# One load per tile over all partitions, the scores in two PSUM tiles, the last table products behind the first expert's products

## The chip, the cores and the metric

The kernel runs on one core of a Trainium2 chip. The metric is the time of one execution on the device in microseconds (us); the median of the runs counts. TensorE is PE in the profile, VectorE DVE, ScalarE ACT, GpSimd POOL; SyncE (SP) issues most transfers here.

## The reference

A causal linear attention with a decay per channel, then a mixture of experts with one expert per row and a skip gate. Cut to what matters:

```python
x = attention(q, k, v, alpha)      # B, H, S, D = 4, 8, 768, 48; x is 3072 x 384
for t in range(S):
    state = alpha[:, :, t, :, None] * state + np.einsum('bhd,bhe->bhde', k[:, :, t], v[:, :, t])
    y[:, :, t] = np.einsum('bhd,bhde->bhe', q[:, :, t], state)
...
do_compute = x @ w_skip > 0        # D, E, F = 384, 8, 1024
logits = x[do_compute] @ w_gate
e_idx = np.argmax(logits, axis=1)  # gate_w: the softmax value of that expert
...
for e in range(E):
    h = np.maximum(xc[e_idx == e] @ w1[e], 0.0)
    y[e_idx == e] = gate_w * (h @ w2[e])
out[do_compute] = xc + y           # all other rows: out = x
```

## The kernel before

**Tiles.** Attention is cut into 24 tiles (NT) of 128 tokens: tile i is chunk i // 4 of batch i % 4, with all eight heads. A tile lies in one of six buffers (`qkv0` to `qkv5`, NQ = 6) of 1932 floats per partition (TW): 524 of decays with guards (`alpha`, AW), 512 of k, 512 of q and 384 of v. For alpha, k and q two heads stand on partitions 0 to 47 and 64 to 111 (PD = 112 in all), four pairs of heads beside each other; v has its 128 tokens on the partitions.

**Loads.** `load` brings the first six tiles' alpha, k and q from `first` over 112 partitions, later ones from `tiles` in two transfers over 48 partitions each, and v in a transfer of its own. All are issued by SP in the order of the code, each waiting there until its part of the buffer is free, and so are the stores of x, the weight pieces (`raw`) and the copies of zeros.

**A tile's steps.** DVE scans the decays backward (`suffix`, `sfx`) and forward (`prefix`, `pfx`); POOL scales k and q by them (`scale_k`, `scale_q`). PE forms the scores (`scores`, 16 products into `ps_s`), half of which ACT copies out (`take_scores`) and POOL masks (`mask_left`), while DVE masks the other half as it copies it (`mask_right`). PE transposes k (`turn_k`, `ps_k`, copied by ACT to `kt`), and adds up y from the old state (`inter`), and from the scores and v (`intra`) in `ps_y`; `outer` and `carry` bring the state on (`ps_v`, then DVE). ACT copies y out as `xt` (`take_y`). One turn later PE multiplies xt by `xw` (`rows`), which gives x as rows and the nine logits (expert gates and skip) in `ps_g`; DVE reduces the logits (`take_logits`) and ACT copies x (`take_x`), which SP stores.

**Order.** Each engine runs its instructions in the order of the code; there is no planner. The loop of `attention` runs the stages of several tiles in one turn i: load i+5, store i-2, scores i+1, prefix and scale_q i+2, inter i, mask_right, turn_k and mask_left i+1, suffix i+3, rows, take_logits and take_x of i-1, scale_k i+3, outer, intra, carry and take_y i. Between them stand jobs that are dealt out in pieces: `route_group` (the routing of tiles 0 to 7, 8 to 14 and 15 to 19; its `one_hot` runs on ACT as two steps, `far` and `hot`, and its `marks` are products on PE that add each row's number and gate to the table `tab`), `weight_pieces` (SP loads w1 and w2 in pieces) and `split_pieces` (ACT rounds a piece to `w1h` or `w2h`, POOL subtracts it to get the rest, `w1l` or `w2l`).

**Tail.** Tiles 20 to 23 are routed one by one (`route_one`). The first expert's rows are gathered by products with one-hots (`late_rows`, `early_turn`) and copied to `xx` (`first_turn`). After that the last two tiles' one-hots, marks and table additions follow, then `indices` (row numbers for the gathers), the gates and the gathers (POOL, `xr`) for experts 1 and 0.

**Experts.** For each of eight experts `up` multiplies (72 products of `ps_h` in four groups), `turn` transposes the next expert's gathered rows (`ps_x`), and `down` multiplies back (48 products of `ps_o`), adds the gated result to x and scatters the rows. `must_redo` forms a flag from the decays that tells whether tiles must be computed again another way.

## Time and profile before

| | us |
|---|---|
| median of 3 runs | 315.44 (314.89 to 315.59) |
| the profiled execution | 314.29 |
| its span | 312.6 |
| PE, DVE, POOL, ACT busy | 284.1, 205.9, 151.3, 141.8 |

The span runs from the first to the last instruction of the profiled execution; 1.7 us lie around it. Its mean granted TensorE clock was 0.919 of full speed. Tile i's start can be read by the start of its scores on PE (line 254): tile 2 at 18.45 us, tile 12 at 67.62, tile 23 at 139.37; the experts begin at 163.76. Busy shares of the whole span are means over these stages and are to be read stage by stage.

### The profile page before, as it was taken

What the parts mean: (1) busy time and instruction counts of PE and PEld (TensorE: products, weight loads), DVE (VectorE), ACT (ScalarE), POOL (GpSimd) and SP (SyncE); (2) the same over time, 40 slices, a digit from 0 to 9 for tenths busy, and PEclk for the clock granted to TensorE, in tenths of its full rate; (3) what the DMA queues carried; (4) which work ended last, traced back from release to release, by engine and by line L of the source; (5) the groups of instructions that cost most, each with busy time, mean ns of one, the idle gap of its engine ahead of it and who ended that gap; (6) DMA issues with size and microseconds to landing.
All of it is one profiled execution on the core that took longest, in us unless ns stands there. A gap on an engine that the chain in (4) does not pass through costs nothing.

```text
span 312.6 us, 7251 instructions
## 1 busy us (share of the span) xinstructions
PE 284.1 (91%) x2831; PEld 265.9 (85%) x2831; DVE 205.9 (66%) x398; ACT 141.8 (45%) x290; POOL 151.3 (48%) x176
## 2 busy tenths in 40 slices
PE   8768999979889979978949999999999999999991
PEld 8557888868778768866939999999999999999991
DVE  5579878896554975884554667675867679575510
ACT  4222555554873567333313827264563817264200
POOL 6287888978676776655127160331414050301111
PEclk9857999995987997996778999999999999999998
DMA  7899999999998892534203355576664756660000
GB/s 203 219 249 199 261 242 282 214 206 229 259 257 228 187 230 86 173 126 113 99 26 97 123 178 206 219 262 226 226 227 130 235 189 209 226 226 25 11 26 21
DMA packets 22793, 55.88 MB, mean 179 GB/s; under 512 B 3896, under 2 KB 10621, under 8 KB 22752
## 3 DMA queue, kind: packets, MB, share of 16 engines
q1 hardware_dynamic: 20576, 50.27, 58.2%
q0 software_dynamic: 2176, 5.08, 4.8%
q8 instruction: 24, 0.39, 0.6%
q14 instruction: 17, 0.14, 0.2%
HBM read 48.30 MB, written 8.65 MB: 182 GB/s over the span
## 4 chain that ended last, share of the span: by engine, by line
PE 61%; DMA 18%; DVE 10%; ACT 4%; POOL 3%; issue 2%; SPq 1%; POOLq 0%; DVEq 0%; ACTq 0%
PE ps_h L633 23%; PE ps_o L648 21%; DMA qkv<-in_tiles_dram 9%; DVE sfx L214 4%; DMA qkv<-in_v_dram 3%; DMA out_dram<-x 3%; DMA qkv<-in_first_dram 3%; PE ps_s L254 3%; PE ps_y L311 2%; PE ps_g L338 2%; PE ps_y L291 2%; PE ps_x L613 1%; PE ps_v L466 1%; DVE pfx L224 1%; PE ps_k L275 1%
## 5 line engine op out<-in xcount | busy, mean ns | idle before, releaser
L653 POOL DMA_INDIRECT out_dram<-o,idx x16 | 22.8, 1424 | 97.6 <-DVE o L651 97.6
L633 PE MATMUL ps_h<-xx,w1h 128*128 128x256 f32 x384 | 59.7, 286 | 0.4 <-DVE tab L471 0.4
L633 PEld LDWEIGHTS ps_h<-xx,w1h 128*128 128x128 f32 x384 | 52.9, 194 | 0.5 <-issue 0.5
L637 ACT ACTIVATE hh<-ps_h 128x512 fp32r<-128x512 f32 x32 | 19.1, 597 | 71.0 <-PE ps_h L633 65.5
L648 PE MATMUL ps_o<-w2h,hh 128*128 128x384 f32 x128 | 43.4, 339 | 0.0
L648 PE MATMUL ps_o<-w2h,hl 128*128 128x384 f32 x128 | 42.9, 335 | 0.0
L648 PE MATMUL ps_o<-w2l,hh 128*128 128x384 f32 x128 | 42.8, 334 | 0.0
L230 POOL TENSOR_TENSOR qkv<-qkv,sfx 112x512 f32<-112x512 f32 x24 | 28.4, 1182 | 23.8 <-DVE sfx L214 21.7
L254 PE MATMUL ps_s<-qkv 48*128 48x128 f32 x384 | 31.3, 308 | 5.2 <-POOL qkv L234 2.8
L638 DVE SCALAR_TENSOR_TENSOR hl<-ps_h,hh 128x512 fp32r<-128x512 f32 x32 | 22.1, 691 | 20.1 <-ACT hh L637 19.1
L254 PEld LDWEIGHTS ps_s<-qkv 48*128 48x128 f32 x384 | 26.5, 210 | 10.2 <-issue 4.1
L633 PE MATMUL ps_h<-xx,w1l 128*128 128x256 f32 x192 | 34.9, 287 | 0.0
L214 DVE TENSOR_TENSOR_SCAN sfx<-qkv,ps_d 112x524 f32<-112x524 f32 x24 | 29.7, 1236 | 7.5 <-DMA qkv<-in_first_dram 6.1
L311 PE MATMUL ps_y<-st,qkv 128*48 128x128 f32 x384 | 33.0, 314 | 0.0
L268 DVE COPY_PREDICATED st<-mask,ps_s 128x512 f32<-128x512 uint8 x24 | 17.6, 734 | 22.3 <-ACT st L260 22.2
L651 DVE SCALAR_TENSOR_TENSOR o<-ps_o,gates,xr 128x384 f32<-128x384 f32 x16 | 9.9, 618 | 30.2 <-PE ps_o L648 30.2
L224 DVE TENSOR_TENSOR_SCAN pfx<-qkv,ps_d 112x524 f32<-112x524 f32 x24 | 29.6, 1234 | 0.1
L633 PEld LDWEIGHTS ps_h<-xx,w1l 128*128 128x128 f32 x192 | 28.7, 196 | 0.0
L349 ACT COPY x<-ps_g 128x384 f32<-128x384 f32 x22 | 10.5, 477 | 38.9 <-DVE ps_d L343 38.9
L338 PE MATMUL ps_g<-xw,xt 112*128 112x105 f32 x176 | 27.3, 305 | 0.8 <-ACT xt L318 0.8
L234 POOL TENSOR_TENSOR qkv<-qkv,pfx 112x512 f32<-112x512 f32 x22 | 26.1, 1186 | 2.6 <-DVE pfx L224 2.4
L586 DVE TENSOR_TENSOR w1l<-raw,w1h 128x768 fp32r<-128x768 f32 x28 | 26.8, 957 | 0.8
(162 smaller groups left out, 552.1 us busy)
## 6 DMA issues: line engine op xcount, KB each, us to landing
raw<-in_w_dram SPq DMA_DIRECT2D x64, 384.0 KB, 4.9
qkv<-in_tiles_dram SPq DMA_DIRECT2D x36, 290.2 KB, 8.9
qkv<-in_v_dram SPq DMA_DIRECT2D x24, 192.0 KB, 8.3
...
```

Of the source, the lines that this page charges most:

```text
L214: nc.vector.tensor_tensor_scan(sfx[:PD][:, ::-1], w["alpha"][:PD][:, ::-1], self.c_r[:PD].to_broadcast([PD, AW]), LOW, ALU.mult, ALU.max)
L224: nc.vector.tensor_tensor_scan(pfx[:PD], w["alpha"][:PD], self.c_f[:PD].to_broadcast([PD, AW]), 0.0, ALU.mult, ALU.max)
L230: (eng or self.nc.gpsimd).tensor_tensor(w["kh"][:PD], w["kh"][:PD], w["sfx"][:PD, :, 3:SEG], ALU.mult)
L234: (eng or nc.gpsimd).tensor_tensor(w["qh"][:PD], w["qh"][:PD], w["pfx"][:PD, :, 2:2 + P], ALU.mult)
L254: nc.tensor.matmul(self.ps_s[:, h, p * P:(p + 1) * P], lhsT=kh[r, p, :], rhs=qh[r, p, :], start=True, stop=True)
L311: nc.tensor.matmul(self.y_out(i, p, h), lhsT=w["v"][:, o:o + D], rhs=w["st"][:, h, p * P:(p + 1) * P], start=(i < B and p < 2), stop=(p >= 2))
L338: nc.tensor.matmul(pg[:, p, :], lhsT=w["xt"][:PD, p, :], rhs=self.xw[:PD, p, :], start=True, stop=True)
L586: (nc.gpsimd if early else nc.vector).tensor_tensor(lo[:, s], raw[:, s], hi[:, s].bitcast(F32), ALU.subtract)
L633: nc.tensor.matmul(ps[:, u, :], lhsT=a[:, k, f * P:(f + 1) * P], rhs=xx[:, k, b, :], start=(n == 0), stop=(n == len(order) - 1))
L638: nc.vector.scalar_tensor_tensor(out=hl, in0=ps, scalar=0.0, in1=hh.bitcast(F32), op0=ALU.max, op1=ALU.subtract)
L648: nc.tensor.matmul(ps, lhsT=a[:, f, js], rhs=b[:, f, :], start=(n == 0), stop=(n == 3 * FT - 1))
L653: ins = nc.gpsimd.indirect_dma_start(out=self.out[:, :], out_offset=bass.IndirectOffsetOnAxis(ap=self.idx[:, e, j:j + 1], axis=0), in_=o, ...
```

## The change

- **Loads.** One input `tiles` of 24 x 128 x 1932 floats, zero where no head lies. A tile is one transfer over 128 partitions, instead of three. At the start tile 0 comes in four pieces, tile 1 in three and tile 2 in two, tile 2's alpha ahead of tile 0's v.
- **Scores.** `ps_s` becomes two tiles of PSUM, one for each half of the scores.
- **Order in the loop.** `take_x` stands ahead of `take_logits`. `route_constants` moves from turn 1 to 3, and its DVE part, on PSUM instead of SBUF, to turn 5. The weight pieces of expert 0 are issued in even turns from 4 on instead of every turn from 3 on, its splits run from turn 9 instead of 6.
- **Tail.** The marks of the last two tiles, their addition to the table, the indices, the gates and the gathers stand in `finish_table`, behind the first quarter of the first expert's products, with `all0` and `all1` as the one-hots.
- **Small.** `must_redo` takes one set of operations over 112 partitions instead of two; the sum of a group's counts lies in PSUM; `hot` has five buffers instead of six.

```diff
@@ -99,7 +99,7 @@
         bank = st.enter_context(tc.tile_pool(name="bank", bufs=1, space=PSUM))
-        self.ps_s = bank.tile([P, 2, NP * P], F32, name="ps_s")
+        self.ps_s = [bank.tile([P, NP * P], F32, name=f"ps_s{h}") for h in range(2)]
         self.ps_y = bank.tile([P, 2, 4 * P], F32, name="ps_y")
@@ -165,11 +165,6 @@
         nc.gpsimd.tensor_copy(self.slots, num)
-        nc.vector.tensor_copy(self.iota, self.slots)
-        self.rank = const.tile([P, E], F32, name="rank")
-        for t in (self.rank, self.rev):
-            nc.vector.tensor_scalar(out=t, in0=self.slots[:, 0:E], scalar1=-1.0, scalar2=float(E + 1),
-                                    op0=ALU.mult, op1=ALU.add)
         self.m = const.tile([P, NT, E], BF16, name="m")
@@ -182,6 +177,15 @@
+    def route_constants_2(self):
+        nc = self.nc
+        nc.vector.tensor_copy(self.iota, self.slots)
+        self.rank = self.const.tile([P, E], F32, name="rank")
+        for t in (self.rev, self.rank):
+            nc.vector.tensor_scalar(out=t, in0=self.iota[:, 0:E], scalar1=-1.0, scalar2=float(E + 1),
+                                    op0=ALU.mult, op1=ALU.add)
     def warm_up(self, n):
@@ -198,14 +202,8 @@
                                 qh=cut(QO, NP * P).rearrange("p (a t) -> p a t", t=P), v=cut(VO, DM))
-        for a, b in cuts or ((0, VO), (VO, TW)):
-            if a == VO:
-                nc.sync.dma_start(out=t[:, VO:], in_=self.v[i])
-            elif i < NQ:
-                nc.sync.dma_start(out=t[:PD, a:b], in_=self.first[i, :, a:b])
-            else:
-                for h in range(2):
-                    nc.sync.dma_start(out=t[64 * h:64 * h + D, a:b], in_=self.tiles[i - NQ, h, :, a:b])
+        for a, b in cuts or ((0, TW),):
+            nc.sync.dma_start(out=t[:, a:b], in_=self.tiles[i, :, a:b])
@@ -251,13 +249,13 @@
                 r = slice(64 * h, 64 * h + D)
-                nc.tensor.matmul(self.ps_s[:, h, p * P:(p + 1) * P], lhsT=kh[r, p, :], rhs=qh[r, p, :],
+                nc.tensor.matmul(self.ps_s[h][:, p * P:(p + 1) * P], lhsT=kh[r, p, :], rhs=qh[r, p, :],
                                  start=True, stop=True)
...
         w = self.work[i]
-        self.nc.scalar.copy(out=w["st"][:, 0, :], in_=self.ps_s[:, 0, :])
+        self.nc.scalar.copy(out=w["st"][:, 0, :], in_=self.ps_s[0])
@@ -413,16 +411,16 @@
         yield nc.vector.tensor_reduce(out=r1, in_=eq, op=ALU.add, axis=AX.X)
-        add = self.sm.tile([P, E], F32, name="add")
+        add = self.ps_d[:, 224:224 + E]
         yield nc.vector.tensor_reduce(out=add, in_=m.rearrange("p n e -> p e n"), op=ALU.add, axis=AX.X)
-        yield nc.vector.tensor_tensor(self.cnt, self.cnt, add, ALU.add)
+        yield nc.vector.tensor_tensor(self.cnt, add, self.cnt, ALU.add)
         w = n if g1 == LATE else 4
...
                 yield
-            ps, Vq = self.ps_v[:, 192:192 + 2 * 3 * E], V[:, q:min(q + w, n), :]
+            ps, Vq = self.ps_v[:, 192:192 + 2 * 3 * E], [V[:, k, :] for k in range(q, min(q + w, n))]
             yield from self.defer(lambda: self.marks(ps, hots, Vq))
@@ -439,16 +437,22 @@
         n = g1 - g0
-        V = self.sm.tile([P, 8, 3 * E], F32R, name="V")[:, :n, :]
+        if g0 >= LATE:
+            V = self.x0.tile([P, 1, 3 * E], F32R, name=f"V{g0}")
+        else:
+            V = self.sm.tile([P, 8, 3 * E], F32R, name="V")[:, :n, :]
         self.nc.gpsimd.tensor_tensor(V.rearrange("p n (e c) -> p n e c", c=3),
...
-    def one_hot(self, r1, eng=None):
-        nc = self.nc
-        hot = self.sm.tile([P, CAP], F32R, name="hot", bufs=6)
+    def one_hot(self, r1, eng=None, late=None):
+        nc = self.nc
+        if late is None:
+            hot = self.sm.tile([P, CAP], F32R, name="hot", bufs=5)
+        else:
+            hot = self.x0.tile([P, CAP], F32R, name=f"all{late % 2}")
         if eng is not None:
@@ -515,10 +519,10 @@
         yield
-        hot = self.one_hot(r1, nc.vector)
+        w["mark"] = [self.one_hot(r1, nc.vector, i)], [V[:, 0, :]]
         yield
         ps = w["pg"][:, 436:436 + 2 * 3 * E]
-        yield from self.defer(lambda: self.marks(ps, [hot], V))
+        yield from self.defer(lambda: self.marks(ps, *w["mark"]))
         yield self.add_marks(ps)
@@ -601,6 +605,17 @@
         self.ew.setdefault(e, {}).update(xr=xr)
+    def finish_table(self):
+        ps = self.ps_f.tile([P, 2 * 3 * E], F32, name="ps_f")
+        self.marks(ps, *self.last_marks)
+        self.add_marks(ps)
+        self.idx = self.indices(0, E, "idx")
+        for n in (1, 0):
+            self.gather(n)
+        self.gate = self.const.tile([P, NB, E], F32, name="gates")
+        self.nc.vector.tensor_tensor(self.gate, self.tab[:, :, :, 1], self.tab[:, :, :, 2], ALU.add)
@@ -864,9 +877,9 @@
         self.load(0, (0, AW), (KO, QO), (QO, VO))
-        self.load(1, (0, AW))
+        self.load(1, (0, AW), (KO, VO))
+        self.load(2, (0, AW))
         self.load(0, (VO, TW))
-        self.load(1, (KO, VO))
         self.constants()
@@ -877,7 +890,8 @@
         self.load(1, (VO, TW))
-        for i in range(2, NQ - 1):
+        self.load(2, (KO, TW))
+        for i in range(3, NQ - 1):
             self.load(i)
@@ -898,14 +912,14 @@
                 self.store(i - 2)
-            if i == 3:
+            if i == 4:
                 fetch = self.weight_pieces(0)
...
                 fetch = self.weight_pieces(1)
-            advance(fetch, 1 if i < 19 else 2)
+            advance(fetch, 2 if i >= 19 else 1 if i % 2 == 0 else 0)
             if LATE <= i + 5 < NT:
                 self.clear(i + 5)
-            if i == 6:
+            if i == 9:
                 split = self.split_pieces(0, early=True)
@@ -922,14 +936,16 @@
             self.tick(2)
-            if i == 1:
+            if i == 3:
                 self.route_constants()
+            if i == 5:
+                self.route_constants_2()
             if i + 3 < NT:
...
                 self.rows(i - 1)
+                self.take_x(i - 1)
                 self.take_logits(i - 1)
-                self.take_x(i - 1)
             if i + 3 < NT:
@@ -956,7 +972,7 @@
         a, b = NT - 2, NT - 1
-        self.x0t = [self.ps_s[:, 0, :CAP], self.ps_s[:, 1, :CAP], self.ps_v[:, 256:256 + CAP]]
+        self.x0t = [self.ps_s[0][:, :CAP], self.ps_s[1][:, :CAP], self.ps_v[:, 256:256 + CAP]]
         for i in range(LATE, a):
@@ -980,22 +996,15 @@
         advance(solo[a - 1], 2)
-        advance(solo[a], 6)
-        advance(solo[b], 7)
-        self.flush()
-        advance(solo[a], 2)
-        advance(solo[b], 2)
-        self.idx = self.indices(0, E, "idx")
-        self.gate = self.const.tile([P, NB, E], F32, name="gates")
-        nc.vector.tensor_tensor(self.gate, self.tab[:, :, :, 1], self.tab[:, :, :, 2], ALU.add)
+        advance(solo[a], 5)
+        advance(solo[b], 6)
+        self.last_marks = [self.work[a]["mark"][n] + self.work[b]["mark"][n] for n in range(2)]
         advance(fetch, 8)
...
         self.ew[0] = dict(xx=self.xx0)
-        for n in (1, 0):
-            self.gather(n)
         for e in range(E):
@@ -1003,6 +1012,8 @@
                 self.up(e, g)
+                if (e, g) == (0, 0):
+                    self.finish_table()
                 advance(split)
@@ -1037,16 +1048,15 @@
     tiles[:, :, :D, QO:VO] = heads(q).reshape(NT, 2, D, NP * P)
-    first = tiles[:NQ].reshape(NQ, P, VO)[:, :PD]
-    tiles = tiles[NQ:, :, :D]
-    vt = v.reshape(B, H, C, P, D).transpose(2, 0, 3, 1, 4).reshape(NT, P, DM)
+    tiles = tiles.reshape(NT, P, TW)
+    tiles[:, :, VO:] = v.reshape(B, H, C, P, D).transpose(2, 0, 3, 1, 4).reshape(NT, P, DM)
     w9 = np.concatenate([moe_w_gate, moe_w_skip[:, None]], axis=1).reshape(NP, 2, D, E + 1).transpose(1, 2, 0, 3)
...
     w2 = moe_w2.reshape(E, FT, P, DM).transpose(0, 2, 1, 3).reshape(E, P, FT * DM)
-    return [np.ascontiguousarray(a) for a in (first, tiles, vt, w9, w1, w2, nat, w9n)]
+    return [np.ascontiguousarray(a) for a in (tiles, w9, w1, w2, nat, w9n)]
```

ACT around one tile's turn in the middle of the loop, before; a name behind "waits" is the engine or the transfer queue that the row waits for.

```order
L260 COPY st_103<-ps_s 128x512 [waits PE_49,Pool_49]
L238 COPY ends<-pfx 112x4 [waits DVE_49]
L277 COPY kt<-ps_k 128x448 [waits PE_49,Activation_49]
L349 COPY x<-ps_g 128x384 [waits DMAHW7_49,DVE_49]
L436 CAST idg<-gate 128x8
L585 CAST w1h<-raw 128x512 [waits DMAHW3_49]
L318 COPY xt_108<-ps_y 112x2x2x128 [waits PE_49,Activation_49]
```

After, on the same engine in the same place:

```order
L258 COPY st_104<-ps_s_90 128x512 [waits PE_49,Pool_49]
L236 COPY ends<-pfx 112x4 [waits DVE_49]
L275 COPY kt<-ps_k 128x448 [waits PE_49,Activation_49]
L347 COPY x<-ps_g 128x384 [waits DMAHW4_49,PE_49]
L434 CAST idg<-gate 128x8 [waits DVE_49]
L589 CAST w1h<-raw 128x512 [waits DMAHW2_49]
L316 COPY xt_109<-ps_y 112x2x2x128 [waits PE_49,Activation_49]
```

The copy of x (now line 347) waits for PE where it waited for DVE. DVE in the same place, before:

```order
L268 COPY_PREDICATED st_103<-mask,ps_s 128x512 [waits Activation_49]
L214 SCALAR_TENSOR_TENSOR sfx<-qkv_101,ps_d 112x524 [waits DMAHW7_49,DMAHW0_49,Pool_49]
L218 RECIPROCAL qkv_101<-sfx 112x4 [waits DVE_49]
L343 TENSOR_REDUCE ps_d<-ps_g 128x9 [waits PE_49]
L388 TENSOR_REDUCE mx<-ps_d 128x8 [waits DVE_49]
```

After, on the same engine in the same place:

```order
L266 COPY_PREDICATED st_104<-mask,ps_s_91 128x512 [waits PE_49]
L212 SCALAR_TENSOR_TENSOR sfx<-qkv_102,ps_d 112x524 [waits DMAHW0_49,Pool_49]
L216 RECIPROCAL qkv_102<-sfx 112x4 [waits DVE_49]
L341 TENSOR_REDUCE ps_d<-ps_g 128x9 [waits Activation_49]
L386 TENSOR_REDUCE mx<-ps_d 128x8 [waits DVE_49]
```

The logits' reduction (line 341) waits for ACT instead of PE, the mask (line 266) for PE instead of ACT, and the suffix scan for one transfer instead of two. PE at the end of the tail, before (`ps_g` and `ps_k` are the table products of the last two tiles, `ps_h` the first expert's):

```order
L466 MATMUL ps_g<-V,hot 128x24 [waits DVE_49,Pool_49]
L466 MATMUL ps_g<-V,hot 128x24
L466 MATMUL ps_k<-V,hot 128x24 [waits DVE_49,Pool_49]
L466 MATMUL ps_k<-V,hot 128x24
L633 MATMUL ps_h<-xx_2041,w1h 128x256 [waits DVE_49,Activation_49]
```

After, on the same engine in the same place:

```order
L533 MATMUL ps_v<-hot_1992,latel_1959 128x256
L648 MATMUL ps_h<-xx_2000,w1h 128x256 [waits DVE_49,Activation_49]
L648 MATMUL ps_h<-xx_2000,w1l 128x256
...
L648 MATMUL ps_h<-xx_2000,w1l 128x256
L648 MATMUL ps_h<-xx_2000,w1h 128x256 x6
L470 MATMUL ps_f<-V_2015,all_2017 128x24 [waits Pool_49]
L470 MATMUL ps_f<-V_2026,all_2028 128x24 [waits Pool_49]
L470 MATMUL ps_f<-V_2015,all_2017 128x24
```

The table products, four in `ps_f`, stand behind 18 of the first expert's products instead of ahead of them.

## Rows read from the trace of the kernel before

**Rows 1.** Windows: length; busy PE, PEld, DVE, ACT, POOL; clock; DMA share; GB/s.

```profile
7.30:35.30 28.00, 22.05 (x254) 19.26 (x254) 21.83 (x33) 8.31 (x21) 17.77 (x25) 0.76 0.98 223
35.30:62.70 27.40, 27.40 (x459) 23.82 (x458) 22.28 (x43) 15.07 (x35) 24.29 (x28) 1.00 1.04 250
62.70:139.40 76.70, 67.43 (x934) 58.55 (x933) 54.00 (x115) 43.38 (x104) 54.67 (x64) 0.89 0.80 202
...
163.80:306.00 142.20, 142.15 (x1004) 141.63 (x1004) 90.83 (x133) 65.14 (x102) 40.38 (x31) 0.99 0.49 167
```

**Rows 2.** Chain of waits at the start: start, duration, what.

```profile
8.67 5.71 DMA qkv<-in_first_dram
14.40 1.26 DVE sfx L214
...
18.45 2.08 PE ps_s L254 x16
```

**Rows 3.** Timeline, DVE and PE at 23 to 32 us: start, duration, engine, line.

```profile
23.83 2.20 DVE L171 TENSOR_SCALAR rank<-slots 128x8 f32<-128x8 f32 x1
...
25.81 1.58 PE L254 MATMUL ps_s<-qkv 48*128 48x128 f32 x16
...
31.27 1.16 PE L254 MATMUL ps_s<-qkv 48*128 48x128 f32 x16
```

**Rows 4.** Waits, 62.7 to 139.4: who for whom: total us, times, longest.

```profile
ACT x L349 <- DVE ps_d L343: 21.6, 12, 2.8
DVE st L268 <- ACT st L260: 15.4, 9, 3.1
...
PE ps_y L291 <- ACT xt L318: 7.5, 7, 1.7
```

**Rows 5.** Timeline, 68 to 117 us; in brackets idle before, and its releaser.

```profile
68.78 0.48 ACT L349 COPY x<-ps_g 128x384 f32<-128x384 f32 x1 [2.82 <-DVE ps_d L343]
...
70.41 0.66 PE L291 MATMUL ps_y<-qkv,old 48*48 48x128 f32 x16 [1.63 <-ACT xt L318]
...
91.09 0.69 PE L291 MATMUL ps_y<-qkv,old 48*48 48x128 f32 x16 [1.43 <-ACT xt L318]
...
116.60 0.66 PE L291 MATMUL ps_y<-qkv,old 48*48 48x128 f32 x16 [1.68 <-ACT xt L318]
```

**Rows 6.** Windows at the half clock between 62.7 and 139.4 us.

```profile
71.10:77.90 6.80, 6.80 (x63) 6.22 (x65) 4.86 (x10) 2.45 (x5) 5.38 (x7) 0.50 1.04 224
91.60:98.40 6.80, 6.80 (x64) 6.14 (x58) 3.73 (x6) 2.98 (x7) 6.32 (x8) 0.50 0.84 218
118.90:122.30 3.40, 3.40 (x33) 3.21 (x34) 2.53 (x7) 2.27 (x6) 2.19 (x4) 0.50 0.00 0
```

**Rows 7.** Windows by transfers: stores and v, then 48-partition loads alone.

```profile
99.00:100.00 1.00, 1.00 (x23) 0.81 (x15) 0.43 (x1) 0.64 (x2) 0.39 (x1) 1.00 0.88 320
101.00:103.00 2.00, 2.00 (x39) 1.87 (x38) 1.90 (x7) 0.48 (x1) 0.73 (x1) 1.00 1.08 223
```

**Rows 8.** Groups by line, ACT, 62.7 to 139.4: busy us, mean ns, idle before.

```profile
L585 ACT CAST w2h<-raw 128x512 fp32r<-128x512 f32 x6 | 3.6, 608 | 0.0
```

**Rows 9.** Timeline of the tail, 159 to 165 us.

```profile
159.10 0.42 DVE L550 CAST xx<-ps_s 128x256 fp32r<-128x256 f32 x1 [1.30 <-ACT xx L550]
...
161.83 0.47 DVE L453 TENSOR_SCALAR hot<-ps_d,r 128x256 fp32r<-128x256 f32 x1
...
162.76 0.60 PE L466 MATMUL ps_k<-V,hot 128*128 128x24 f32 x2 [0.25 <-DVE tab L471]
...
164.31 1.04 POOL L556 DMA_INDIRECT xr<-out_dram,idx  x1 [1.60 <-DVE gates L990]
```

**Rows 10.** Chain of waits at the first expert.

```profile
163.76 10.14 PE ps_h L633 x72
...
173.90 0.66 PE ps_x L613 x6
```

**Rows 11.** Gathers of xr between 163 and 172 us, from issue to landing.

```profile
DMA to landing us min/median/max: 3.7/3.7/3.7
```

28 lines of the change are left out of this document (13 added, 15 removed).

## Prediction

> **What bounds the kernel now.** I read the windows by stage first, because the share of busy time over the whole span (PE 91%) mixes stages with different limits. [rows 1] shows four stretches. In the first, 7.30 to 35.30, PE works 22.05 of 28.00 us and the DMA share is 0.98: the pipeline fills and is fed by transfers. From 35.30 to 62.70 PE works all 27.40 us (six tiles, 4.57 us each): nothing but PE counts there. From 62.70 to 139.40 it works 67.43 of 76.70, at a mean granted clock of 0.89. From 163.80 on, the experts, it works 142.15 of 142.20. So only the first and third stretch, and the short tail ahead of 163.8, can give time back by better feeding.
>
> Then the chain of waits for the first stretch [rows 2]: the load of tile 2 is issued at 8.67 and takes 5.71 us; tile 2's suffix scan starts as it lands (14.40), and scan, scaling and scores follow, so that PE's scores of tile 2 start at 18.45. Then the timeline there [rows 3]: two operations of 8 columns keep DVE 2.20 us from 23.83, ahead of tile 4's suffix scan, and the scores of tiles 3 and 4 start 31.27 - 25.81 = 5.46 us apart.
>
> Then the waits of the third stretch [rows 4]: ACT idles 21.6 us ahead of its copy of x for DVE's logits, DVE 15.4 us ahead of its mask for ACT's copy of the scores; they wait for each other although neither needs the other's result. PE's own large wait is that for xt, ACT's last copy of a tile: 7.5 us in seven times. [rows 5] shows the link: at 68.78 ACT starts x after 2.82 us idle, and 1.6 us later PE starts `inter` after waiting 1.63 us for xt. The last two rows there are two more of the seven. [rows 6] shows what follows: three stretches at 0.50 of the full clock (1.2 instead of 2.4 GHz), beginning 0.7, 0.5 and 2.3 us after those three waits ended, PE busy throughout. 17.0 us at half speed hold 8.5 us of work, so they cost 3.4 + 3.4 + 1.7 = 8.5 us.
>
> **The change part by part.**
> *The loads.* A tile was 2 x 297 KB over 48 partitions and 197 KB over 128; it is 989 KB over 128 partitions, 198 KB more, 24 x 198 KB = 4.75 MB in all, with one issue instead of three. Rates: while loads over 48 partitions ran alone, 223 GB/s at a share of 1.08; with the share at 0.88 in a microsecond of transfers over 128 partitions, 320 [rows 7]. In the PE-bound stretch the new need is 989 KB, a store and on average one weight piece of 197 KB each, 1,383 KB per 4.57 us = 303 GB/s. The new loads resemble the second row, so 320 to 360 are there and I charge nothing; with the first row's rate it is the first rival.
> The Trainium skill ("SBUF — State Buffer", section "Door 1: The DMA port swizzle (why `[64,N]` ≈ `[32,N]`)") says that a transfer's rate goes by how many of 16 ports its partitions reach, and 48 partitions of one half reach eight. An estimate from that page would be 594/218 + 197/435 = 3.2 us per tile before and 989/435 = 2.3 after; the 223 GB/s row agrees with its first half, no row here shows the second for a whole load.
> A load now also waits for v's reader, `intra` of the tile before, one loop turn ahead; the five spare buffers cover that: nothing, and 5.71 us once if not.
> *The start.* The decays of tile 2 are now loaded ahead of the first v. Their scan no longer starts at 14.40 but when DVE is done with tiles 0 and 1, at about 11.2; 14.40 to 18.45 is 4.05 us of scan, scalings and scan, which gives scores at 15.2, or 16.8 if k and q, in the second transfer, come last. Gain 1.7 to 3.2, I take 2.8. The constants move out: tile 4's scan loses up to 2.2 us of delay; the interval falls from 5.46 toward the steady 4.57, and a little below it if tile 3 comes later than that scan allowed before: 0 to 2.2, I take 1.5. Start **4.3 (1.7 to 5.4)**. The constants' DVE part goes to loop turn 5, where DVE works 22.28 of 27.40 us and PE has a full queue [rows 1]: nothing; without that cover 2.2.
> *x ahead of the logits.* ACT's copy of x waits for PE instead of DVE; DVE's reduction waits for ACT instead of PE. Queued behind ACT's copy are routing one-hots, the weight splits (0.608 us) [rows 8] and xt, so xt comes earlier by as much as ACT was kept idle just before. Of PE's 7.5 us the five waits with such idle time ahead can go by 0.3, 1.5, 0.75, 0.3 and 0.9, about 3.7; the other two, one of them behind one-hots, stay. Range 2 to 6. Queued behind DVE's new wait are the state update, the next prefix scan and the next mask, for which `inter` and the scores wait; ACT stood ready for that copy in 12 cases, 21.6 us in all [rows 4], so nothing, at worst one x copy of 0.48 us [rows 5] in each of 12 tiles: 6.
> *Scores in two tiles of PSUM.* Removes DVE's 15.4 us of waiting; DVE is not what PE waits for there and has 22.7 us to spare, so nothing by itself: the work it hides behind is PE's.
> *The clock.* With the waits at 70.41, 91.09 and 116.60 shortened to some 0.1, 0.7 and 0.8 us, the first half-clock stretch has lost the wait that stood ahead of it, the others half of theirs. Between 0 and 8.5 I count one: 3.4.
> *Weights later.* Splits run in turns 9 to 20 instead of 6 to 17: three more fall where the one-hots of the second and third group crowd ACT, 0.6 us of ACT each [rows 8], and some of POOL. 0 to 3.2 lost; I take 1.2.
> Middle: 3.7 + 3.4 - 1.2 = **5.9 (0 to 12)**.
> *Late and tail.* For the last tiles the logits now come one x copy later, 0.48 [rows 5]: -0.4. The last one-hot starts at 161.83 and ends at 162.30, the table products take 0.60 a pair [rows 9] and the first expert's products start at 163.76 [rows 10]. These no longer stand behind the table, which saves 1.46; DVE's copy for them at 159.10 waited 1.30 for ACT's, of which 0.42 go. But the two pairs now run inside the PE-bound stage: 1.9 - 1.2 = 0.7. The gathers were issued from 164.31, 0.55 after the products' start. Now 18 of 72 products come first (2.5 us by 10.14/4, twice that at the half clock, I take 3.8), 1.2 of table products and the 0.95 from their end to the issue: 5.9 after. The second, 1.04 on, lands 3.7 later [rows 11], at 10.6; the turn that needs it came at 173.90 - 163.76 = 10.1 [rows 10], now 11.3. It just holds; at 5.1 it is 0.6 late. Tail and late **0.3 (-0.8 to 0.7)**. must_redo's fewer operations lie under PE-bound products: nothing.
>
> **Sum.** 4.3 + 5.9 + 0.3 = 10.5. The profiled execution took 314.29 us (span 312.6, 1.7 around it); it would take 303.8. The median of the runs, 315.44, is 1.15 above it, so I predict 304.9, put as 305.0.
>
> **The rivals.**
> *Bytes (slower).* If 128 partitions do not raise the rate, only the 25% remain. From 7.30 to 139.40 the queue moved 28.00 x 223 + 27.40 x 250 + 76.70 x 202 = 28.6 MB in 132.1 us [rows 1], with a mean share near 0.89: 243 GB/s at a full share. 33.3 MB at that rate take 137.0 us, 4.9 longer, and the start gain is lost in it: 315.44 + 4.9 - 0.3 = 320.0. It decides against the kernel below 33.3/132.1 = 252 GB/s, and costs part of the gain below 273. For it: the share is near 1 until 62.7 now. Against: 320 GB/s in [rows 7].
> In the skill's page "DMA: Bandwidth & Descriptors", section "Anatomy of one DMA — SWDGE (gpsimd) path", a transfer costs 2.0 us and its bytes at 436 GB/s; by that, as an estimate, 198 KB are 0.45 us more per load and no rate improves with the shape. The two rows of [rows 7] disagree with one rate for all shapes.
> *The one-hots and splits keep ACT late (less faster).* The waits for xt shrink, but all three half-clock stretches stay: 4.3 + 3.7 - 1.2 + 0.3 = 7.1, so 308.3, and with the low end of the start 310.9. For it: one of the seven waits stands without idle time on ACT, and the splits come later.
> *All three stretches go (more faster).* 4.3 + 3.7 + 8.5 - 1.2 + 0.3 = 15.6: 299.8. For it: each follows one of these waits.
> *Nothing comes of it.* The start gain is given back as an earlier arrival at the next wait, the swap only moves the wait from ACT to DVE: 315.4. Against: PE never waits from 35.3 to 62.7, so what the start gains is kept that far.
>
> **How the numbers follow.** Forecast, 302 to 308: 0.43. ACT late, 308 to 312: 0.25. All stretches gone, 297 to 302: 0.17. Bytes, 317 to 323: 0.08. Nothing: 0.07, of which 0.03 within 0.2% (about what a measurement of this kernel can tell from no change), 0.03 faster, 0.01 slower. Faster 0.43 + 0.25 + 0.17 + 0.03 = 0.88, same 0.03, slower 0.09. The range leaves out bytes, most of nothing and the far end of the stretches, 0.2: 298 to 312.
>
> **What would show it.** Scores of tile 2 near 15 to 16 and of tile 4 near 27 us; no DMA share at 1 with PE idle before 60 us; loads at 300 GB/s or more. ACT's wait of x for DVE gone, DVE's wait of the logits for ACT short; PE's wait for xt at some 4 us; two half-clock stretches left between 62 and 130 us. The first expert's products ahead of the table products, the turn to the second expert without a wait for the gathered rows. Wrong it is if the suffix scans wait for loads in the middle, if stretches at the half clock stand in new places, or if the late splits hold xt.

## The result, and the profile after

The changed kernel takes 301.35 us (median of 4 runs, 299.96 to 304.61) against 315.16 for the kernel before beside it (4 runs): a ratio of 0.9552, 95% interval 0.9506 to 0.9598, 14 us. The forecast was 305.0, with a range of 298 to 312. Its profiled execution took 301.59 us with a span of 299.9, against 314.29 and 312.6. Runs of one kernel differ by 2 to 3% with the TensorE clock they were granted (31 further runs of the kernel before: 310.66 to 318.47 us), so four to six runs do not tell 2 us apart; the ratios leave out runs more than 1.5% above the fastest of their kernel, and the profiled executions of a_48h, a_joint, a_flush, a_earlyw and a_same below were among the slower ones of their kernels, so that lengths of stages in them are those of one execution.

The first part of the page: busy time of each engine, its share of the span, and instructions.

```profile
PE 278.0 (93%) x2831; PEld 260.0 (87%) x2831; DVE 201.4 (67%) x393; ACT 142.9 (48%) x290; POOL 152.1 (51%) x176
```

PE runs the same 2831 products, in 278.0 us instead of 284.1. Of the 12.7 us that the span lost, 6.1 are therefore busy time of PE, and the other 6.6 are its idle time: 312.6 - 284.1 = 28.5 before, 299.9 - 278.0 = 21.9 after. Of the 6.1, 1.1 saved nothing: the products of zeros ahead of tile 0 take 5.31 us instead of 6.38, at the full clock in both, and PE then waits 1.00 us for DVE. First row before, then two after:

```profile
0.85 6.38 PE L189 MATMUL ps_y<-const-float32-0.0 128*128 128x128 f32 x32 [0.85 <-PEq L1057]
```

```profile
0.85 5.31 PE L193 MATMUL ps_y<-const-float32-0.0 128*128 128x128 f32 x32 [0.85 <-PEq L1067]
7.16 1.16 PE L252 MATMUL ps_s<-qkv 48*128 48x128 f32 x16 [1.00 <-DVE qkv L232]
```

In the stages behind them, the table below, 5.0 us are products that ran at a higher clock and 7.6 are idle time. The forecast's sum, sorted the same way, was 3.4 for the clock and 4.3 + 3.7 - 1.2 + 0.3 = 7.1 for waits. The windows by stage, cut at the same places in the work as [rows 1] (columns as there; the fourth row is the tail):

```profile
7.20:29.15 21.95, 20.11 (x254) 17.64 (x254) 19.61 (x31) 9.12 (x22) 15.60 (x22) 0.84 0.92 332
29.15:56.80 27.65, 27.45 (x457) 23.84 (x456) 23.30 (x46) 14.36 (x32) 23.36 (x28) 1.00 0.91 303
56.80:125.80 69.00, 63.40 (x933) 54.81 (x931) 51.72 (x113) 44.16 (x105) 57.59 (x67) 0.93 0.74 245
125.80:150.20 24.40, 18.67 (x154) 16.25 (x153) 12.10 (x69) 6.93 (x23) 7.77 (x14) 0.70 0.24 76
150.20:293.30 143.10, 143.05 (x1008) 142.23 (x1008) 90.47 (x130) 65.22 (x102) 41.56 (x32) 0.99 0.48 166
```

| stretch | before | after | gain | of it PE busy | of it PE idle |
|---|---|---|---|---|---|
| start | 28.00 | 21.95 | 6.05 | 1.94 | 4.11 |
| steady | 27.40 | 27.65 | -0.25 | -0.05 | -0.20 |
| middle | 76.70 | 69.00 | 7.70 | 4.03 | 3.67 |
| tail | 24.40 | 24.40 | 0.00 | -0.03 | 0.03 |
| experts | 142.20 | 143.10 | -0.90 | -0.90 | 0.00 |

The transfers show in the last columns: 332 and 303 GB/s at a share of 0.92 and 0.91, where [rows 1] has 223 and 250 at 0.98 and 1.04. In these two stretches the 25% more bytes go through with less of the transfer engines' time.

Waits of the middle, 56.8 to 125.8 us (who for whom: total us, times, longest), beside [rows 4]:

```profile
ACT x L347 <- PE ps_g L336: 6.5, 8, 2.2
...
DVE st L266 <- PE ps_s L252: 4.1, 5, 1.4
...
PE ps_y L289 <- ACT xt L316: 3.7, 5, 1.1
```

The two engines no longer wait for each other; both wait for PE. PE's wait for xt has gone from 7.5 to 3.7 us.

### The profile page after: what moved, and what is told of

It is laid out like the page before. It is cut to its first block, busy times and chain, and to the rows that moved or that the text cites. A ratio compares the mean times of both kernels' runs of the same rounds, so it can differ in the third digit from the quotient of the medians.

```text
span 299.9 us, 7149 instructions
## 1 busy us (share of the span) xinstructions
PE 278.0 (93%) x2831; PEld 260.0 (87%) x2831; DVE 201.4 (67%) x393; ACT 142.9 (48%) x290; POOL 152.1 (51%) x176
## 4 chain that ended last, share of the span: by engine, by line
PE 82%; DVE 9%; ACT 4%; POOL 2%; issue 1%; DMA 1%; POOLq 0%; DVEq 0%
PE ps_h L648 23%; PE ps_o L663 22%; PE ps_s L252 8%; PE ps_y L309 6%; PE ps_g L336 6%; PE ps_y L289 4%; PE ps_v L301 3%; PE ps_k L273 3%; PE ps_v L470 2%; DVE sfx L212 2%; PE ps_x L628 2%; DVE pfx L222 2%; ACT far L460 1%; PE ps_k L336 1%; DMA qkv<-in_tiles_dram 1%
## 5 line engine op out<-in xcount | busy, mean ns | idle before, releaser
L228 POOL TENSOR_TENSOR qkv<-qkv,sfx 112x512 f32<-112x512 f32 x24 | 28.5, 1187 | 11.5 <-DVE sfx L212 9.2
L252 PE MATMUL ps_s<-qkv 48*128 48x128 f32 x384 | 30.6, 300 | 3.0 <-DVE qkv L232 2.8
L252 PEld LDWEIGHTS ps_s<-qkv 48*128 48x128 f32 x384 | 25.8, 201 | 8.0 <-issue 5.5
L309 PE MATMUL ps_y<-st,qkv 128*48 128x128 f32 x384 | 31.8, 306 | 0.0
L560 POOL DMA_INDIRECT xr<-out_dram,idx x18 | 22.0, 1225 | 13.4 <-DVE gates L618 5.6
L589 ACT CAST w1h<-raw 128x768 fp32r<-128x768 f32 (+1 forms) x34 | 26.8, 789 | 0.0
L309 PEld LDWEIGHTS ps_y<-st,qkv 128*48 128x48 f32 x384 | 24.9, 138 | 0.6 <-issue 0.4
```

The source lines that it names most:

```text
L228: (eng or self.nc.gpsimd).tensor_tensor(w["kh"][:PD], w["kh"][:PD], w["sfx"][:PD, :, 3:SEG], ALU.mult)
L252: nc.tensor.matmul(self.ps_s[h][:, p * P:(p + 1) * P], lhsT=kh[r, p, :], rhs=qh[r, p, :], start=True, stop=True)
L309: nc.tensor.matmul(self.y_out(i, p, h), lhsT=w["v"][:, o:o + D], rhs=w["st"][:, h, p * P:(p + 1) * P], start=(i < B and p < 2), stop=(p >= 2))
L589: nc.scalar.copy(out=hi[:, s], in_=raw[:, s])
```

## The experiments

Letters: a_ is the changed kernel with one thing undone or added, b_ the kernel before with one part of the change alone. Ratios are to the kernel before on the same chip, with 95% intervals.

**a_noswap**, the order of x and logits undone:

```diff
-                self.take_x(i - 1)
                 self.take_logits(i - 1)
+                self.take_x(i - 1)
```

> The changed kernel with the logits' reduction ahead of the copy of x again. Theory 1 (the swap is what keeps xt from being late, and with it the clock): ACT waits again some 15 to 20 us for DVE's logits between 60 and 130 us, PE waits 6 to 8 us for xt there, half-clock time between 60 and 122 us rises from 6.8 us to about 17: 3.7 + 5 us lost, 308 to 311 us. Theory 2 (the wide loads made the gain of the middle too): within 1.5 us of the changed kernel, 300 to 303 us.

304.96 us (4 runs, 304.09 to 306.31), 0.9689 (0.9622 to 0.9757). The waits of its middle, 57.3 to 130.3 us:

```profile
ACT x L347 <- DVE ps_d L341: 16.4, 10, 2.3
...
PE ps_y L289 <- ACT xt L316: 5.1, 5, 1.7
```

and its windows by stage in the middle:

```profile
57.27:130.28 73.01, 65.69 (x933) 57.03 (x932) 52.88 (x113) 44.08 (x106) 57.58 (x67) 0.91 0.72 235
```

Beside the row of after, 69.00 us with 63.40 busy, the stretch is 4.0 longer: 2.3 of products at a lower clock, and 1.7 of idle time, 1.4 of it the wait for xt. A second trace of the changed kernel, a_same below, has 64.08 us busy there, so some 0.7 of the 2.3 lies between executions of one program. The mechanism of theory 1 stands, at half its size: 3.6 us of 8 to 9, with 5.1 us of waiting for xt where 6 to 8 were expected. Theory 2 missed.

**b_swap**, the same order put into the kernel before.

```diff
+                self.take_x(i - 1)
                 self.take_logits(i - 1)
-                self.take_x(i - 1)
```

> The kernel before with the copy of x ahead of the logits' reduction, alone. Theory 1: ACT's 21.6 us of waiting for the logits go, PE's wait for xt falls from 7.5 to about 4 us, and one or two of the half-clock stretches go: 306 to 310 us. Theory 2: the loads still set the pace: 313 to 316 us.

313.08 us (4 runs, 309.46 to 319.72), 0.9871 (0.978 to 0.9963). Its waits between 62 and 136 us:

```profile
PE ps_y L291 <- ACT xt L318: 4.2, 5, 2.2
```

PE's wait fell from 7.5 to 4.2 as theory 1 said, the time by 1.3% only, where 1.7 to 2.9% were expected, which puts the median into theory 2's range; its runs lie 10 us apart, and how much of the clock this order gives is not settled by it.

**b_128**, the wide loads alone, in the old order at the start:

```diff
-        for a, b in cuts or ((0, VO), (VO, TW)):
...
-                    nc.sync.dma_start(out=t[64 * h:64 * h + D, a:b], in_=self.tiles[i - NQ, h, :, a:b])
+        for a, b in cuts or ((0, TW),):
+            nc.sync.dma_start(out=t[:, a:b], in_=self.tiles[i, :, a:b])
```

> The kernel before with the wide loads alone (one transfer of 128 partitions and 989 KB per tile, from one input), in the old order at the start. Theory 1: tile 2 still stands behind the first v's, its load of 989 KB lands some 1 us earlier than before, the rest does not matter: 313 to 315 us. Theory 2: most of the gain comes by this alone: 303 to 308 us. If the added 25% of bytes limit the loads: 318 to 322 us.

312.5 us (10 runs, 310.17 to 314.2), 0.9914 (0.9872 to 0.9956): just below theory 1's range, and far from both others. Tile 11's scores start at 63.29 us in its trace, against 62.69 before: with the old order and the constants in turn 1, faster loads bring nothing to the start. The ten runs are still 0.9% faster (0.4 to 1.3%); where that comes from its one trace, 0.4 us shorter than that of the kernel before, does not show.

**a_48**, the old cut of the loads in the changed kernel.

```diff
-        for a, b in cuts or ((0, TW),):
-            nc.sync.dma_start(out=t[:, a:b], in_=self.tiles[i, :, a:b])
+        for a, b in cuts or ((0, VO), (VO, TW)):
+            if a == VO:
+                nc.sync.dma_start(out=t[:, VO:], in_=self.tiles[i, :, VO:])
+            elif i < NQ:
+                nc.sync.dma_start(out=t[:PD, a:b], in_=self.tiles[i, :PD, a:b])
+            else:
+                for h in range(2):
+                    r = slice(64 * h, 64 * h + D)
+                    nc.sync.dma_start(out=t[r, a:b], in_=self.tiles[i, r, a:b])
```

> The changed kernel with its loads cut as before: alpha, k and q over 112 partitions for the first six tiles, then in two transfers over 48 partitions, v by itself; the order of the loads at the start stays the new one. Theory 1: the order at the start keeps most of its gain and the loads lie under PE's work after that: 1 to 3 us lost, 302 to 305 us. Theory 2: the loads were the limit, transfers run at about 220 GB/s again, tiles land late and suffix scans wait for them: 8 to 12 us lost, 309 to 313 us.

A miss of the experiment: 6062 us. Rows 48 to 63 of a buffer are no longer loaded from the seventh tile on, the changed `must_redo` looks at all 112 rows, raises its flag, and every tile is computed a second time in the other way. So the two edits belong together: one set of operations for the flag is only possible since the padding rows come with each load.

**a_48h**, the same with the flag taken from the two halves:

```diff
+            for h in range(2):
+                r = slice(64 * h, 64 * h + D)
...
+                nc.vector.tensor_scalar(out=self.oddb[r], in0=least[r], scalar1=0.5, scalar2=None, op0=ALU.is_lt)
```

> The changed kernel with its loads cut as before (48 partitions twice, and v; 112 partitions for the first six tiles), the start in the new order, and the flag taken from the two halves apart as before, so that rows 48 to 63 don't count. If the start's gain is only kept because the wide loads keep up (new theory): scores of tile 6 wait for a load, tile 12 starts at 66 to 67 us instead of 61.4, 5 us lost: 305 to 308 us. If the loads lie under PE's work (theory 1): 301 to 303 us.

304.23 us (4 runs, 302.15 to 308.22), 0.9602 (0.9527 to 0.9678). Its windows by stage, start and steady, and rows of its timeline:

```profile
7.56:30.90 23.34, 20.59 (x253) 17.63 (x254) 17.85 (x27) 9.07 (x22) 13.84 (x15) 0.85 1.01 226
30.90:63.60 32.70, 30.67 (x457) 26.68 (x457) 25.09 (x50) 14.26 (x32) 25.14 (x35) 0.90 1.02 265
```

```profile
30.60 1.25 DVE L219 TENSOR_TENSOR_SCAN sfx<-qkv,ps_d 112x524 f32<-112x524 f32 x1 [0.39 <-DMA qkv<-in_tiles_dram]
...
32.64 2.10 POOL L178 MEMSET xr<- 128x768 f32 x3
...
36.32 1.20 POOL L239 TENSOR_TENSOR qkv<-qkv,pfx 112x512 f32<-112x512 f32 x1
...
37.56 1.47 PEld L259 LDWEIGHTS ps_s<-qkv 48*128 48x128 f32 x16 [2.29 <-POOL qkv L239]
37.57 1.76 PE L259 MATMUL ps_s<-qkv 48*128 48x128 f32 x16 [2.03 <-DMA qkv<-in_tiles_dram]
```

DVE's waits for loads from 8 to 64 us, here and after:

```profile
DVE sfx L219 <- DMA qkv<-in_tiles_dram: 5.1, 4, 3.0
```

```profile
DVE sfx L212 <- DMA qkv<-in_tiles_dram: 1.3, 1, 1.3
```

The transfers are back at 226 GB/s with a full share. PE waits 2.03 us ahead of the scores of tile 6. The last row names a transfer, but tile 6's own data had landed when its suffix scan began at 30.60; what ends at 36.32 + 1.20 = 37.52, 0.05 ahead of the scores, is POOL's scaling of tile 6's q, which PEld's row names. POOL came to it late because the routing constants, now in turn 3, hold it from 31.39 to 34.74, and it came late to those because the scans of tiles 3 to 6 each waited for their load, 5.1 us in all instead of 1.3. So the old loads cost time one step further back than the expectation had it. After the wait, 0.5 us later a half-clock stretch begins; the steady part, 27.65 us in the changed kernel, takes 32.70, of which 3.2 are products at a lower clock and 1.8 idle time. Tile 11 starts at 63.60, later than before the change. The time of all runs shows less of it, 1 to 3 us beside the changed kernel, with intervals that overlap: the step is seen in the trace, its price in the time is only bounded.

**a_const1**, all routing constants back in turn 1:

```diff
-            if i == 3:
+            if i == 1:
                 self.route_constants()
-            if i == 5:
                 self.route_constants_2()
```

> The changed kernel with all the routing constants back in turn 1. Prediction's step: DVE's two small operations cost tile 4 about 1.5 us (0 to 2.2), the rest of the start stays: 302 to 303.5 us. Rival, from tile 4 of the kernel with the wide loads alone (7.55 us after tile 3, against 3.98): the constants block DVE and POOL for 3.5 us and that is the larger part of the start's gain: 304 to 306 us.

301.66 us (4 runs, 300.4 to 302.49), 0.954 (0.9477 to 0.9602). Tile 4 starts at 27.26 instead of 25.15, and tile 11 at 58.66 instead of 56.82: 1.84 us lost by the trace, near the prediction's 1.5. But its step is not what the trace has. The edit puts back the place of the constants and not their operand, so that DVE's two operations read PSUM and take 0.17 us each instead of the 2.20 of [rows 3]:

```profile
22.59 0.17 DVE L186 TENSOR_SCALAR ps_d<-ps_d 128x8 f32<-128x8 f32 x1
22.80 0.17 DVE L186 TENSOR_SCALAR rank<-ps_d 128x8 f32<-128x8 f32 x1
```

```profile
16.90:23.60 6.70, 6.70 (x58) 5.93 (x58) 4.58 (x9) 2.28 (x5) 5.09 (x11) 0.50 0.78 326
```

What is lost is lost in this half-clock stretch: tile 3 comes 6.72 us after tile 2 instead of 4.38, with PE busy throughout. Whether the constants have to do with it is open, and neither expectation is tested. The time is that of the changed kernel. The middle of the trace:

```profile
58.66:124.70 66.04, 59.52 (x933) 51.38 (x932) 51.26 (x113) 43.97 (x105) 57.47 (x67) 1.00 0.79 260
```

No half-clock stretch fell into it, and that gave back 3.0 us in this trace. A microsecond at the start is less than what the clock does later.

**a_joint**, both halves of the scores in one tile of PSUM:

```diff
-        self.ps_s = [bank.tile([P, NP * P], F32, name=f"ps_s{h}") for h in range(2)]
+        self.ps_s = bank.tile([P, 2, NP * P], F32, name="ps_s")
```

> The changed kernel with both halves of the scores in one tile of PSUM again. Prediction's step: DVE waits some 15 us for ACT's copy of the scores in the middle, but PE does not wait for DVE, so nothing is lost before the tail, and some 0.4 us there: 301 to 302.5 us. Rival: DVE's lost time delays the scans and with them the scores, 3 us or more and a half-clock stretch: 304 to 308 us.

304.01 us (4 runs, 300.56 to 306.5), 0.9533 (0.9443 to 0.9623). Waits of its middle, 57.6 to 128.4:

```profile
DVE st L266 <- ACT st L258: 11.0, 8, 2.8
...
PE ps_y L289 <- ACT xt L316: 3.4, 4, 1.1
```

DVE's wait is back, PE's is what it was: in the trace the split alone gives PE nothing. The time does not settle it: two runs, 300.56 and 302.11, fit the expectation, two, 305.91 and 306.5, the rival.

**a_flush**, the third group's table products behind the scores of tile 23 (turn 22) instead of ahead of them:

```diff
-            if i == LATE + 1:
+            if i == LATE + 2:
                 self.flush()
                 self.tick(3)
```

> The changed kernel with the table products of the third group behind the scores of tile 23 instead of ahead of them. In the changed kernel PE idles 1.35 us for DVE's one-hots just ahead of these products, and a half-clock stretch of 17 us begins 0.5 us after. If that wait is what the stretch follows: the stretch goes or halves, 4 to 8 us gained: 293 to 298 us. If the clock there falls for another reason (less work for PE on the whole in this stage): 0.5 to 1.3 us gained, 300 to 301 us.

299.56 us (4 runs, 295.66 to 301.34), 0.9435 (0.9347 to 0.9524). Timeline of PE around it, then windows of two of its half-clock stretches:

```profile
122.21 1.16 PE L252 MATMUL ps_s<-qkv 48*128 48x128 f32 x16 [0.82 <-POOL qkv L232]
123.31 1.75 PE L470 MATMUL ps_v<-V,hot 128*128 128x24 f32 x10
124.98 0.66 PE L289 MATMUL ps_y<-qkv,old 48*48 48x128 f32 x16
126.55 0.17 PE L506 MATMUL ps_g<-m,tri 128*128 128x8 bf16 x1 [0.91 <-DVE m L502]
```

```profile
126.60:140.00 13.40, 11.74 (x81) 10.21 (x81) 5.18 (x32) 3.71 (x12) 5.04 (x9) 0.50 0.15 50
147.10:153.70 6.60, 5.04 (x23) 5.07 (x24) 1.45 (x9) 1.15 (x4) 0.85 (x4) 0.50 0.01 1
```

The 1.35 us wait is gone and tile 23 starts 3.6 us earlier. The stretch did not go: it moved from 123.5 to 126.5, where PE had just waited 0.91 us for DVE, and is 13.4 instead of 17.0 us long. In the eight traces of changed kernels that have these products ahead of tile 23's scores, such a stretch begins between 2.3 us before those scores and 1.4 after (a_same: 127.4, 1.0 after, 13.6 us long); here it begins 4.3 after. So the order moves it, but that it became shorter is not shown. Nor is the one wait that it follows: in a_fill below, with the same order, it begins at 124.1, ahead of the end of the wait for DVE at 125.40. 1.1 to 1.8 us gained beside the two medians of the changed kernel (300.67 below, 301.35), about the smaller expectation; the intervals overlap.

**a_same, a_tab1st, a_earlyw, a_fill** ran side by side, six runs each.

> The changed kernel itself, once more, as the measure for the other three on the same chip: 301 us, 300 to 304, with a mean granted clock of 0.93 to 0.95.

300.67 us (298.66 to 302.51), 0.9584 (0.9516 to 0.9653). The middle of its trace, a second one of the changed kernel:

```profile
57.20:126.40 69.20, 64.08 (x933) 55.58 (x931) 51.69 (x113) 44.44 (x105) 57.48 (x67) 0.93 0.76 246
```

a_tab1st, the table ahead of the first products:

```diff
         self.ew[0] = dict(xx=self.xx0)
+        self.finish_table()
...
-                if (e, g) == (0, 0):
-                    self.finish_table()
```

> The changed kernel with the last two tiles' table products, additions, indices and gathers ahead of the first expert's products again. Prediction's step: the deferral saves 1.9 of waiting and costs 1.2 inside the products, so 0.7 us lost without it: 301.7 to 302.5 us, the first expert's products 1.4 to 1.9 us later against the last tile's scores and 1.2 us shorter. Rival: the first products wait for the last one-hot anyway and nothing is gained: within 0.4 us of the changed kernel.

300.42 us (298.65 to 301.23), 0.9586 (0.9522 to 0.965): by the time, the rival. Its tail and experts:

```profile
123.40:149.00 25.60, 19.87 (x158) 17.41 (x157) 12.09 (x69) 6.94 (x23) 7.99 (x15) 0.63 0.23 72
149.00:291.50 142.50, 142.49 (x1005) 142.00 (x1005) 90.43 (x129) 65.13 (x102) 39.76 (x31) 0.99 0.49 167
```

The traces have the prediction's step: the first products come 25.6 us after tile 23's scores instead of 24.4 (23.8 in a_same), and the experts' stage is shorter, 142.5 instead of 143.1 (143.4). Together 168.1 beside 167.5 (167.2): by the traces the deferral is worth 0.6 to 0.9 us, where 0.7 was forecast. Six runs do not tell that from nothing.

a_earlyw, weight pieces and splits as before:

```diff
-            if i == 4:
+            if i == 3:
                 fetch = self.weight_pieces(0)
...
-            advance(fetch, 2 if i >= 19 else 1 if i % 2 == 0 else 0)
+            advance(fetch, 1 if i < 19 else 2)
...
-            if i == 9:
+            if i == 6:
                 split = self.split_pieces(0, early=True)
```

> The changed kernel with the weight pieces of expert 0 in turns 3 to 10 and their splits from turn 6, as before. Prediction's step: the later splits cost 1.2 us (0 to 3.2), so 0 to 3 us are gained back: 298 to 301 us. Rival: the early pieces stand in the stretch where loads keep the DMA share above 0.9, so tiles land late, 1 to 4 us lost: 302 to 305 us.

298.23 us (295.44 to 300.92), 0.948 (0.9404 to 0.9556), 2.4 us less than the changed kernel by the medians. PE's wait for xt between 56.6 and 125 us:

```profile
PE ps_y L289 <- ACT xt L316: 2.5, 3, 1.1
```

2.5 us instead of 3.7; but one program gives 3.0 (a_same) to 4.4 us (a_tab1st, unchanged up to there). Tiles do not land late (its steady part moves 325 GB/s at a share of 0.95), so the rival is out. That the later places are a loss inside the change, as the prediction's step says, is the likelier reading of the two medians; the intervals overlap, and the edit moves the loads of the pieces as well as the splits, so it is not shown.

a_fill, a_flush with products of zeros in front of the tail's two waits:

```diff
+            self.nc.tensor.matmul(self.ps_y[:, 0, :P], lhsT=zero, rhs=zero, start=True, stop=True)
...
+        self.fill(4)
         for k in range(KT):
             self.late_rows(b, k)
...
+        self.fill(14)
         advance(solo[a - 1], 2)
```

> The changed kernel with the third group's table products behind the scores of tile 23, and 4 and 14 products of zeros that nothing reads ahead of the last rows' gather and of the first expert's products, where PE idles 0.9 and 3.1 us. If the half-clock stretch of 3 to 7 us that lies over the first products follows these two waits: it goes, 1 to 3 us gained against the kernel without the zeros, 296.5 to 298.5 us. If not: 299 to 300.5 us, the zeros costing 0 to 0.5.

298.14 us (295.22 to 301.93), 0.9496 (0.9417 to 0.9576). Window over the first expert's products:

```profile
147.00:154.00 7.00, 6.94 (x60) 6.97 (x61) 3.49 (x8) 2.65 (x5) 2.29 (x3) 1.00 0.04 8
```

The first expert's products, from 147.06 here, run at 1.00; in a_flush, from 148.66, they run at 0.50 (the second window there). In each of the twelve other traces (a_48 aside) a half-clock stretch lies on these products (in after 150.8 to 154.2); a_fill's is the only one without. So the stretch went with the two waits, in one trace; the time is in the expected range, but its interval overlaps those of a_flush and of the changed kernel.

a_fill and a_earlyw, at about 298.2, are the fastest medians; the two edits were not run together.

## Why the prediction was right, and where it was off

**The total.** 10.5 us forecast, 12.7 by the profiles, 14 by the medians: inside the range. By the stages the waits were 7.1 forecast and 7.6 measured, the clock 3.4 forecast and 5.0 measured, from one trace on either side. Of the prediction's bands the measured time lies in that of "all three stretches go" (297 to 302) and just outside its own (302 to 308); but that rival's mechanism did not come about, since half-clock stretches of 3.3 us are left in the middle. The mis-sized term is the clock's: 4.0 for 3.4 in the middle, and 1.9 in the start, where the sum had none. That the waits agree so well is in part luck: 4.1 for 4.3 in the start, 3.7 for 2.5 in the middle, nothing for 0.3 behind it.

**The start: 4.3 (1.7 to 5.4) forecast, 5.9 measured at tile 11** (62.69 to 56.82). PE's scores after, on its timeline:

```profile
16.79 1.56 PE L252 MATMUL ps_s<-qkv 48*128 48x128 f32 x16
21.17 1.16 PE L252 MATMUL ps_s<-qkv 48*128 48x128 f32 x16
25.15 1.16 PE L252 MATMUL ps_s<-qkv 48*128 48x128 f32 x16
```

Tile 2 starts 1.66 earlier than in [rows 2], the low end of 1.7 to 3.2, but not for that end's reason, k and q last: its scan came at 10.97, as forecast, and POOL had scaled k and q by 14.13 + 1.18 = 15.31, near the 15.2 of the other end; no idle time stands before the row, PE itself was late. Tile 4 follows 3.98 after tile 3 instead of 5.46 in [rows 3]: 1.48 for 1.5, and this too by another path. Before, its own q was ready at 29.17 + 1.19 = 30.36, ahead of PE at 31.27; what the interval held was 0.81 us of waiting for xt and a start at half the clock. Both numbers fit by luck. The rows, of after and of before:

```profile
14.13 1.18 POOL L232 TENSOR_TENSOR qkv<-qkv,pfx 112x512 f32<-112x512 f32 x1
```

```profile
28.73 1.14 PE L338 MATMUL ps_g<-xw,xt 112*128 112x105 f32 x8 [0.81 <-ACT xt L318]
...
29.17 1.19 POOL L234 TENSOR_TENSOR qkv<-qkv,pfx 112x512 f32<-112x512 f32 x1 [0.52 <-DVE pfx L224]
```

What the sum did not have is tile 3, 21.17 - 16.79 = 4.38 after tile 2 instead of 25.81 - 18.45 = 7.36: 2.98 us. There the clock is the difference between these two traces; windows of before and of after:

```profile
13.10:26.70 13.60, 10.78 (x100) 9.58 (x99) 10.03 (x13) 2.33 (x6) 9.06 (x15) 0.50 1.04 241
```

```profile
10.90:17.60 6.70, 6.70 (x59) 5.76 (x59) 5.25 (x9) 1.90 (x4) 3.55 (x5) 0.50 1.01 412
```

Before, all of tile 2's products ran at half the clock, after, only the first of them. I had looked at the three stretches of the middle and not at the one that lay over the start.

But the gain at tile 11 does not hang on that stretch. Rows of a_flush, then of b_swap:

```profile
33.71 1.16 PE L252 MATMUL ps_s<-qkv 48*128 48x128 f32 x16 [1.26 <-POOL qkv L232]
```

```profile
26.52 1.11 PE L338 MATMUL ps_g<-xw,xt 112*128 112x105 f32 x8 [2.47 <-DVE ps_d L343]
```

a_flush, whose code at the start is that of the changed kernel, has no half-clock stretch there and reaches tile 4 at 23.82, 1.33 earlier; but then PE waits 1.26 us ahead of tile 6 for POOL, which the constants now hold in turn 3, and tile 11 comes at 56.55, only 0.27 earlier. b_swap, with the old start, ran tile 3 at the full clock, 3.99 after tile 2, and then waited 2.47 us for DVE's logits, behind the constants: tile 11 at 62.02. With the constants in turn 1, tiles 2 to 4 took 11.1 to 13.1 us (before, b_128, b_swap, a_const1), with them in turn 3 and the wide loads 8.1 to 8.8 (eight traces). So the constants and what they delay seem to be worth more than the 1.5 of the sum; no run undoes them alone together with their operand, so how much is open.

**The loads: charged at nothing.** Right for the changed kernel (PE idle 0.20 of 27.65 us in the steady part, share 0.91), and rival "bytes" is out: the need of 303 GB/s was met at that share. But "nothing" hid what they are worth. In the kernel before they gain nothing at the start (b_128: tile 11 at 63.29) and 0.9% in all; under the faster start the old ones take back all of it in one trace (a_48h: 63.60), 1 to 3 us in the time. The argument against the last rival, that PE never waits from 35.3 to 62.7 and so keeps what the start gains, was read from a trace in which PE came later: with the wide loads it held to 0.20 us in after, while in a_flush PE waits 1.26 us there for POOL, and with the old loads it waits 2.03.

The port rule of the Trainium skill ("SBUF — State Buffer", section "Door 1: The DMA port swizzle (why `[64,N]` ≈ `[32,N]`)") agrees in its direction: 332 GB/s at a share of 0.92 with the wide loads, 226 at 1.01 with the old ones. That the ports are the reason is not shown: the old loads are also three transfers for one, and the first six tiles' lie over 112 partitions, which its table does not have. Its table for transfers of 1 MiB, 328 GB/s over 128 partitions and 196 over 64, lies nearer to these rows than the 435 from which the estimate in the prediction was made; in the one row above with the wide loads at a share of 1.01 they move 412. The fit of 2.0 us and 436 GB/s that the prediction set beside rival "bytes" stands in the Trainium skill ("DMA: Bandwidth & Descriptors", section "Anatomy of one DMA — SWDGE (gpsimd) path") for transfers issued by GpSimd; these are issued by SP, and no run here tests it.

**x ahead of the logits: 3.7 forecast, 3.8 less wait for xt measured** (7.5 to 3.7; 3.3 in b_swap alone). Undoing the order gives back only 1.4 (a_noswap); what else shortened the wait no run shows. The middle's idle time of PE fell by 3.67 where 3.7 - 1.2 had been forecast. The new wait of DVE on ACT cost no PE time that a row shows.

**The clock in the middle: 3.4 forecast, 4.0 measured.** [rows 6] held 17.0 us at half the clock; after, two stretches of 3.3 are left there (3.4 and 6.8 in a_same), and a third begins 2.3 us before tile 23:

```profile
75.70:79.00 3.30, 3.30 (x38) 2.76 (x36) 2.68 (x5) 2.62 (x6) 1.58 (x2) 0.50 0.24 93
109.90:113.20 3.30, 3.30 (x36) 2.84 (x35) 2.71 (x5) 1.00 (x2) 3.30 (x4) 0.50 0.36 82
123.50:140.50 17.00, 15.21 (x113) 12.82 (x113) 6.99 (x41) 3.73 (x12) 5.38 (x9) 0.50 0.31 97
```

The first two stand in the turns of tiles 14 and 20, where those of before stood in 12, 15 and 19: one of the prediction's signs of being wrong. Two runs tie a stretch to what PE does ahead of it: the third begins later when the order of the products changes (a_flush, a_fill), and the one on the first expert's products went, in one trace, when zeros filled two waits (a_fill). That the three of before followed PE's waits is argued, not shown. a_const1, with more idle time in the middle (6.5 us) than after (5.6) and no stretch there at all, and a_same, with waits like those of after and other stretches, speak against a simple rule.

**Tail and late: +0.3 forecast, -0.9 measured.** The 1.46 us between the last one-hot and the first products were saved, but did not stay a gain. Rows of DVE and PE there:

```profile
149.56 0.47 DVE L457 TENSOR_SCALAR all<-ps_d,r 128x256 fp32r<-128x256 f32 x1
...
150.17 0.36 PE L648 MATMUL ps_h<-xx,w1h 128*128 128x256 f32 x1 [3.14 <-DVE all L457]
...
153.65 0.77 PE L470 MATMUL ps_f<-V,all 128*128 128x24 f32 x4
```

The products follow the last one-hot at once, as meant, but that one-hot now ends 150.03 - 125.83 = 24.2 us after tile 23's scores start, against 162.30 - 139.37 = 22.9 before: half the clock lies on 14.7 us of that, up to 140.5, against 10.2 before (139.4 to 146.2 and 149.6 to 153.0). The table products, 0.77, and a slower first quarter lengthen the experts' stage by 0.9. The turn to the second expert waits for nothing: PE is idle 0.05 us in the whole stage.

**Splits later: 1.2 lost forecast (0 to 3.2), 2.4 by the medians of a_earlyw and a_same**, with intervals that overlap. **Two tiles of PSUM: nothing** in PE's waits, as forecast (a_joint); the times leave up to 3 us open.

What stays open: no experiment undid the order of the loads at the start alone, and the single undoings (3.6, 1 to 3, 0, 0 to 3, 0 and -2.4 us) do not add up to 14. That part of the change works only together, and that the clock answers to all of it, is the likely reason and not shown.
